# Expert 0's second layer: from plain products to Strassen's form, for its early and its late tokens

## The chip, the cores and the metric

The kernel runs on one core of one Trainium2 chip. The metric is the device time of one execution in microseconds (us), the median of several. A change under 0.5% (some 2.2 us here) can't be told from none.

Engines: PE (TensorE, the matrix engine) with its weight loads shown apart as PEld; DVE (VectorE); ACT (ScalarE); POOL (GpSimd); SP (SyncE), which issues most of the transfers. Each takes its instructions in the order of the program. DMA engines move data beside them.

## The reference

Linear attention with a decay per head, then a mixture of eight experts, top 1, over the 3072 tokens of width 512:

```python
# attention: B, H, S, D = 4, 8, 768, 64, in blocks of 64 positions
intra = ((qb @ kb.T) * Dmask) @ vb
inter = (qb * lam_pow) @ kv_state
out[block] = intra + inter
kv_state = lam_block * kv_state + (kb * rev_pow).T @ vb
# x: (3072, 512); experts: E = 8, F = 1024
logits = x @ w_gate
expert_idx = argmax(logits);  gate_w = softmax(logits)[expert_idx]
for e in range(8):
    xe = x[expert_idx == e]
    out[expert_idx == e] = gate_w * (maximum(xe @ w1[e], 0) @ w2[e])
```

All is float32.

## The kernel before

**Stages.** The attention runs in 12 steps of 128 positions and two batches. At the end of each step its tokens are routed: their rows are scattered into a list per expert in device memory (`xs`). Then the experts run one after another as "passes", each over a fixed number of tokens (`CAPS`), half of them of even and half of odd place in the list. Expert 0 has two passes: "0a" with 256 tokens that are on its list early (`passes[0]`, called `first`), begun while the attention still ends, and "0b" with the other 130 (`passes[1]`, called `second`). Passes 2 to 8 are the seven other experts, 418 down to 356 tokens.

**The two layers.** The first layer makes `hT`, the hidden values with features on the partitions: 8 chunks of 128 features by the pass's tokens. The second layer is `outputs` for pass 0a (tokens on the output's partitions; the 128 tokens of a chunk of `hT` are the weights that PE holds, 512 columns of `w2t` stream through) and `columns` for pass 0b (128x128 pieces of `w2t` are the held weights, the 130 tokens stream through). In `columns` features are on the partitions, so `put_columns` turns the result back by 32x32 blocks on DVE and writes it to memory, from where `take_rows` reads it as rows for the gates.

**Strassen's form.** Passes 2 to 8 already use it, for both layers. `form` computes a product of 2x2 blocks with seven products of blocks in place of eight. It needs four sums of blocks of each factor (S1 to S4 of the left, T1 to T4 of the right), all made by DVE: `second_sums` for `w2`, `sums_of_hidden` and `last_sum` (S4) for `hT`, `first_sums` for `w1`, `token_sums` for the tokens. Three of the products are added up in one PSUM bank, the `chain`; between them ACT copies the bank out (`snap`), and DVE joins results (`join`, `give`). The order on PE is A11·B11 (chain), A12·B21, S2·T2 (chain), S1·T1, S3·T3 (chain), S4·B22, A22·T4 (chain). `fill(j)` is called after step j, and issues whatever else the engines are to do there. `outputs_fast` is the form for the last pass, with tokens on the partitions; `columns_fast` is that for passes 2 to 7, with tokens streaming.

**What sets the order.** PE, DVE, ACT and SP issue strictly as the code is written. POOL keeps its order too for the scatters. So the order of calls in `experts()` is the order on each engine:

```python
hidden(first, w1t, range(4, FC))       # L1102: last half of 0a's first layer
outputs(first, w2t, between)           # L1109; between(): 0b's rows are cleared, turned
hidden(second, w1t)                    # L1110
prepare(passes[2])                     # L1112: turns pass 2's tokens, token_sums
w1 = first_sums(weights[1][0])         # L1113
columns(second, w2t)                   # L1118
for i in range(2, last + 1): ...       # L1119
```

`w1t` and `w2t` of expert 0 lie by columns: `w2t` is a view [128, 8 chunks, 4 groups, 128], whose groups of 128 columns are stored apart (four dimensions); those of the other experts are [128, 8, 512]. `piece` gives a 128x128 piece of either.

A float32 product of the program is two weight loads and two matmuls in the trace, each with the same shape; a turning by PE (`tr`, L678) is one of each.

Of the kernel before, what the change touches and what calls it, by code (L numbers as in the profile page):

```python
# [10 lines left out]
F32 = mybir.dt.float32  # L11
BF16 = mybir.dt.bfloat16
I32 = mybir.dt.int32
AX = mybir.AxisListType
ALU = mybir.AluOpType
# [6 lines left out]
def kernel(  # L22
# [242 lines left out]

    def piece(wt, c, g):
        return wt[:, c, g] if len(wt.shape) == 4 else wt[:, c, g * P:(g + 1) * P]

    def load_turned(w1t, d):
        for c in range(DC):  # L270
# [16 lines left out]
    def bank(i, shape, name):  # L287
        return ps.tile(shape, F32, tag=f"bank{i}", name=name)
# [372 lines left out]
    def evac(i, dst, src):  # L661
        if i % 2:
            return nc.scalar.copy(dst, src)
        return nc.vector.tensor_copy(dst, src)
# [93 lines left out]
        return left_sums(a, a[1][0], s2, s3, s4)  # L758

    def second_sums(w2t, keep):  # L760
        b = [[w2t[:, j * FC // 2:(j + 1) * FC // 2, k * MD // 2:(k + 1) * MD // 2]
              for k in range(2)] for j in range(2)]
        t1, t2, t4, *t3 = (qkv.tile([P, FC // 2, MD // 2], F32, tag=t, name=f"t_{t}")
                           for t in ("qkvq" if keep else "qkv"))
        return right_sums(b, t1, t2, t3[0] if keep else b[0][1], t4)

# [71 lines left out]
    def columns_fast(m, w2, fill):  # L838

        start_columns(m)  # L840
        mm = quarters(FC // 2, lambda lhs, rhs, fc, i: rhs[:, fc, i * P:(i + 1) * P],
                      lambda lhs, rhs, fc, i: lhs[:, fc, :])

        def give(i, k, p, u):
            to = m.yT[i][:, 2 * k:2 * k + 2, :m.h]
            if u is None:
                nc.scalar.copy(to, p)
            else:
                nc.vector.tensor_add(to, p, u)
            if (i, k) in ((0, 1), (1, 0)):  # L850
                put_columns(m, i)

        form(banks_of(form_banks, [P, 2, m.h]), mm, (m.a, w2), temps_of([P, 2, m.h]), copy_snap,
             nc.vector.tensor_add, give, fill)

    def columns(m, w2t):
        start_columns(m)
        for c in range(0, DC, 2):
            po = bank(next(po_banks), [P, 2, m.n], "po")
            for i, fc in itertools.product(range(2), range(FC)):  # L860
                nc.tensor.matmul(po[:, i, :], lhsT=piece(w2t, fc, c + i),  # L861
                                 rhs=m.hT[:, fc, :], start=(fc == 0), stop=(fc == FC - 1))
            for i in range(2):
                evac(1, m.yT[i][:, c:c + 2, :m.h], po[:, :, i * m.h:(i + 1) * m.h])
        for i in range(2):
            put_columns(m, i)

    def start_columns(m):
        m.y = []
# [35 lines left out]
                             ACT.Copy, scale=m.gates[:w, j, k:k + 1])  # L905
        scatter(m.ids[:w, j, k:k + 1], o[:w])

    def outputs_fast(m, w2t, w2):
        tail_rows(m, w2t)
        last_sum(m)  # L910

        def mm(p, lhs, rhs, first):
            for fc in range(FC // 2):
                nc.tensor.matmul(p, lhsT=lhs[:, fc, :], rhs=rhs[:, fc, :],  # L914
                                 start=(first and fc == 0), stop=(fc == FC // 2 - 1),
                                 skip_group_check=True)

        o = [work.tile([P, MD], F32, tag="kT", name="o") for i in range(2)]
        outs = [[o[i][:, k * MD // 2:(k + 1) * MD // 2] for k in range(2)] for i in range(2)]
        gate = [m.gates[:, 0, i:i + 1] for i in range(2)]  # L920
        ids = ffn.tile([P, 2], I32, name="ids_of_halves", bufs=1)
        nc.vector.tensor_scalar(out=ids[:, 0:1], in0=m.ids[:, 0, 1:2], scalar1=float(N),
                                scalar2=2.0, op0=ALU.min, op1=ALU.mult)
        nc.vector.tensor_scalar(out=ids[:, 1:2], in0=ids[:, 0:1], scalar1=1.0, scalar2=None,
                                op0=ALU.add)

        def snap(j, dst, src):
            nc.scalar.activation(dst, src, ACT.Copy, scale=gate[j == 2])

        def join(dst, p, u):  # L930
            nc.vector.scalar_tensor_tensor(out=dst, in0=p, scalar=gate[0], in1=u,
                                           op0=ALU.mult, op1=ALU.add)

        def give(i, k, p, u):
            if u is None:
                nc.scalar.activation(outs[i][k][:, :P], p[:, :P], ACT.Copy, scale=gate[i])
                nc.vector.tensor_scalar_mul(outs[i][k][:, P:], p[:, P:], gate[i])
            else:
                nc.vector.scalar_tensor_tensor(out=outs[i][k], in0=p, scalar=gate[i], in1=u,
                                               op0=ALU.mult, op1=ALU.add)  # L940
            if i == 1:
                scatter(ids[:, k:k + 1], outs[i][k], out.rearrange("n (k f) -> (n k) f", k=2))
            elif k == 1:
                scatter(m.ids[:, 0, i:i + 1], o[i])

        form(banks_of(form_banks, [P, MD // 2]), mm, (m.a, w2), temps_of([P, MD // 2]), snap, join,
             give, nothing_else)

    def tail_rows(m, w2t):

# [123 lines left out]
    def experts():  # L1074

        total = routed.total
        passes.append(make_pass(0, EARLY, CAPS[0] - EARLY, "0b"))
        load_rows(passes[1])
        for i in range(1, E):
            e = nc.values_load(routed.turns[0:1, i:i + 1], min_val=1, max_val=E - 1,  # L1080
                               engines=[mybir.EngineType.SP])
            passes.append(make_pass(e, 0, CAPS[i], str(i)))
            if i == 1:
                load_meta(passes[2])
                weights.append([load_first(e), None])
        fetch(passes[2])
        weights[1][1] = load_second(passes[2].w)
        last = len(passes) - 1

        def prepare(m):  # L1090
            turn(m)
            token_sums(m)
            for f in m.b.todo:
                f()

        def run_todo(lists, j):
            for f in lists.get(j, ()):
                f()

        w1t, w2t = weights[0]  # L1100
        first, second = passes[:2]
        hidden(first, w1t, range(4, FC))  # L1102

        def between():
            clear_rows(second, place_late, total[:, 0:1])
            turn_rows(second, (2, 3))
            know_rows(second, place_late, total[:, 0:1])

        outputs(first, w2t, between)  # L1109
        hidden(second, w1t)  # L1110
        weights.append([load_first(passes[3].w), None])
        prepare(passes[2])  # L1112
        w1 = first_sums(weights[1][0])  # L1113
        for f in w1.todo:
            f()
        load_meta(passes[3])
        fetch(passes[3])
        columns(second, w2t)  # L1118
        for i in range(2, last + 1):  # L1119
            m = passes[i]  # L1120
            take_rows(passes[i - 1])
            if i < last:
                weights[i][1] = load_second(passes[i + 1].w)
                if i + 2 <= last:
                    load_meta(passes[i + 2])
            else:
                load_tail(m)
            w2 = second_sums(weights[i - 1][1], i == last)
            rows = give_rows(passes[i - 1])
            fills = {j: [f] for j, f in zip((1, 3, 7, 9), w2.todo)}  # L1130
            slots = (10, 13) if i == 2 else (9, 10, 13, 13) if i == last else (9, 10, 13)
            for j, f in zip(slots, rows):
                fills.setdefault(j, []).append(f)
            later = rows[len(slots):]
            hidden_fast(m, w1, i == last, lambda j: run_todo(fills, j))
            know_meta(m, total[:, i - 1:i])
            if i == last:
                know_tail(m, total[:, E - 1:])
                tc.keep_in_program_order(nc.gpsimd.drain())
                outputs_fast(m, weights[i - 1][1], w2)  # L1140
                break
            if i + 2 <= last:
                weights.append([load_first(passes[i + 2].w), None])
            following = passes[i + 1]
            turn(following)
            token_sums(following)
            if i + 2 <= last:
                fetch(passes[i + 2])
            w1 = first_sums(weights[i][0])
            t, w = following.b.todo, w1.todo  # L1150
            fills = {0: later + t[:2], 1: t[2:] + w[:1], 2: [lambda m=m: last_sum(m)] + w[1:2], 3: w[2:3],
                     4: w[3:]}
            columns_fast(m, w2, lambda j: run_todo(fills, j))
# [162 lines left out]
```

## Time and profile before

| | |
|---|---|
| median of 3 runs | 431.95 us (431.32 to 432.99) |
| the profiled execution's own time | 433.69 us |
| its span, first to last instruction | 431.8 us |
| PE busy | 419.5 us, 97% of the span |
| DVE, ACT, POOL busy | 283.5, 151.5, 95.4 us |
| mean granted PE clock | 0.99 of full speed |
| pass 0a, second layer | 137.97 to 152.25 us of the span |
| pass 0b, first layer | 152.25 to 159.41 us |
| pass 0b, second layer | 159.41 to 166.58 us |
| passes 2 to 8 | 166.58 to 424.42 us |

The profile is of one execution. Its chain of work that ended last gives, for each stretch of time, the work that the end waited for; where PE stands there, what PE has to do sets the time. A row of the timeline gives start, length, engine, line, operation, shapes and the number of instructions, and in brackets how long the engine sat idle before and for what. Lengths of PE rows hold the way through the array, so neighbours overlap; the step from one row's start to the next is what an instruction costs.

### The profile page before, as it was taken

Reading aid. Unit: us, or ns where it says so; the run is one execution under the profiler, and the core shown is the slowest. Engines: PE = TensorE matmul, PEld = TensorE weight load, DVE = VectorE, ACT = ScalarE, POOL = GpSimd, SP = SyncE. Lnnn points to the kernel's source line nnn. Section 1 sums busy time; section 2 is a strip of 40 time slices with the busy share of each in tenths; the row PEclk is TensorE's granted clock in tenths of the full one; section 3 lists DMA queues with packets and bytes.
Section 4 is the critical chain, followed back from the end, with each engine's and each line's share of the span. In section 5 each row is a group of like instructions: output and inputs, shape, how many; then the busy total and the mean of one; then the engine's idle time right before and its main releaser. Section 6 shows DMA issues by size and latency. Waiting matters only on the chain.

```text
span 431.8 us, 11052 instructions
## 1 busy us (share of the span) xinstructions
PE 419.5 (97%) x4407; PEld 389.6 (90%) x4407; DVE 283.5 (66%) x678; ACT 151.5 (35%) x370; POOL 95.4 (22%) x122
## 2 busy tenths in 40 slices
PE   8899999999999999999999999999999999999993
PEld 4689999999887499999999999999999999999672
DVE  4677777777744229787569576766957958766601
ACT  3355546555541022430351144025124314413420
POOL 6526545551324000000011003001101200300402
PEclk9899999999999999999999999999999999999997
DMA  9999899988883699764399069539927927604301
GB/s 198 227 214 263 226 250 234 234 211 218 235 268 125 224 332 296 248 233 73 87 330 297 15 185 352 157 85 312 301 44 246 356 49 192 217 0 98 114 26 56
DMA packets 129373, 84.50 MB, mean 196 GB/s; under 512 B 81764, under 2 KB 112244, under 8 KB 129312
## 3 DMA queue, kind: packets, MB, share of 16 engines
q1 hardware_dynamic: 122752, 69.56, 59.0%
q0 software_dynamic: 4464, 13.62, 8.8%
q8 instruction: 37, 0.61, 0.6%
q10 hardware_dynamic: 2096, 0.52, 0.5%
q14 instruction: 24, 0.20, 0.1%
HBM read 64.58 MB, written 19.42 MB: 195 GB/s over the span
## 4 chain that ended last, share of the span: by engine, by line
PE 94%; DVE 2%; DMA 1%; ACT 1%; issue 0%; POOLq 0%; POOL 0%; ACTq 0%
PE p L804 55%; PE tx L450 6%; PE ph L690 5%; PE po L973 3%; PE op L412 3%; PE sp L370 3%; PE p L914 3%; PE tq L313 3%; PE op L390 2%; PE cp L429 2%; PE tk L331 2%; PE op L404 2%; PE po L861 2%; PE po L957 2%; PE sp L375 1%; DMA lam_bc<-in_lam_dram 1%
## 5 line engine op out<-in xcount | busy, mean ns | idle before, releaser
L655 POOL DMA_INDIRECT out_dram<-o,ids x13 | 12.9, 990 | 172.4 <-ACT o L903 170.2
L804 PE MATMUL p<-hT,w2t 128*128 128x209 f32 (+5 forms) x288 | 49.4, 327 | 0.0
L804 PEld LDWEIGHTS p<-hT,w2t 128*128 128x128 f32 x288 | 47.7, 189 | 0.0
L731 ACT COPY u_qsT<-p 128x418 f32<-128x418 f32 (+6 forms) x40 | 19.2, 480 | 77.6 <-PE p L804 76.3
L804 PE MATMUL p<-xgT,w1t 128*128 128x209 f32 (+6 forms) x224 | 38.7, 326 | 0.0
L804 PEld LDWEIGHTS p<-xgT,w1t 128*128 128x128 f32 x224 | 36.7, 190 | 0.0
L829 ACT ACTIVATE hT<-hT 128x418 f32<-128x418 f32 (+6 forms) x42 | 22.0, 525 | 32.9 <-DVE hT L828 32.9
L507 POOL DMA_INDIRECT xs<-x,row x24 | 23.6, 985 | 39.6 <-DVE slot L545 13.9
L380 DVE TENSOR_TENSOR mt<-sp,tables 128x384 f32<-128x384 f32 x48 | 23.6, 549 | 3.4 <-PE sp L375 3.1
L450 PE MATMUL tx<-back,xT 128*128 128x136 f32 x192 | 25.3, 285 | 0.0
L450 PEld LDWEIGHTS tx<-back,xT 128*128 128x128 f32 x192 | 23.1, 190 | 0.8
L828 DVE TENSOR_TENSOR hT<-p,u_qsT 128x418 f32<-128x418 f32 (+6 forms) x28 | 15.5, 558 | 12.2 <-ACT u_qsT L731 9.6
L690 PE MATMUL ph<-xgT,w1t 128*128 128x256 f32 (+1 forms) x128 | 22.0, 328 | 0.2 <-issue 0.2
L690 PEld LDWEIGHTS ph<-xgT,w1t 128*128 128x128 f32 x128 | 19.2, 190 | 2.6 <-issue 0.9
L716 DVE TENSOR_TENSOR u_qsT<-p,u_qsT 128x418 f32<-128x418 f32 (+6 forms) x20 | 11.2, 560 | 15.4 <-PE p L804 15.4
L370 PE MATMUL sp<-qT,kT 64*64 64x128 f32 x384 | 19.8, 276 | 1.4 <-DVE qsT L323 0.8
L804 PE MATMUL p<-t_kd,w1t 128*128 128x209 f32 (+6 forms) x112 | 20.7, 327 | 0.0
L804 PE MATMUL p<-t_xT,s_q 128*128 128x209 f32 (+6 forms) x112 | 20.6, 326 | 0.0
L804 PE MATMUL p<-t_sd,w1t 128*128 128x209 f32 (+6 forms) x112 | 20.5, 326 | 0.0
L804 PE MATMUL p<-xgT,s_v 128*128 128x209 f32 (+6 forms) x112 | 20.5, 326 | 0.0
L804 PE MATMUL p<-xgT,s_k 128*128 128x209 f32 (+6 forms) x112 | 20.5, 326 | 0.0
L670 DVE STREAM_TRANSPOSE xgT<-xb 128x768 f32<-128x768 f32 (+1 forms) x14 | 13.7, 1014 | 10.0 <-PE ph L690 9.9
(239 smaller groups left out, 902.9 us busy)
## 6 DMA issues: line engine op xcount, KB each, us to landing
w1t<-in_moe_w_dram SPq DMA_DIRECT2D x7, 2048.0 KB
w2t<-in_moe_w_dram SPq DMA_DIRECT2D x7, 2048.0 KB
qkv_in<-in_q_dram SPq DMA_DIRECT2D x12, 256.0 KB
q_in<-in_q_dram SPq DMA_DIRECT2D x12, 256.0 KB
y<-ye SPq DMA_DIRECT2D x6, 512.0 KB
xb<-xs SPq DMA_DIRECT2D x32, 96.0 KB
xb<-xs SPq DMA_DIRECT2D x24, 112.0 KB
ye<-yb SPq DMA_DIRECT2D x12, 224.0 KB
```

Source lines behind the costliest of these rows:

```text
L313: nc.tensor.transpose(tq[:, a, b], m.q[:, u, at:at + 2], ident)
L370: nc.tensor.matmul(sp[r][halves[u], b, u:u + 2], lhsT=m.kT[u][halves[r], a, b, halves[u]], rhs=m.qT[u][halves[r], a, b, :], start=(b == 0) ...
L380: nc.vector.tensor_mul(mt[:, r], sp[r], decay[:, r, a].unsqueeze(1).to_broadcast(shp))
L412: nc.tensor.matmul(out_at(m, a, b, u, r)[:, D:], lhsT=m.v[:, u, column(b, a, r), :], rhs=m.mt[a][:, r, b, 2 * u], start=False, stop=(m.n = ...
L450: nc.tensor.matmul(tx[:, b * W:(b + 1) * W], lhsT=m.xT[hp % 2][:, hp // 2, b, :], rhs=back[:, hp, b * E:b * E + W], start=(b == 0), stop=( ...
L507: put = tc.keep_in_program_order(nc.gpsimd.indirect_dma_start(out=xs, out_offset=bass.IndirectOffsetOnAxis(ap=row, axis=0), in_=src, in_of ...
L670: nc.vector.transpose(m.xgT[:, :, i, :].rearrange("p d (b t) -> p b d t", t=Q), m.xb[:, i * nb:(i + 1) * nb].rearrange("p b (d f) -> p b d ...
L690: nc.tensor.matmul(ph, lhsT=piece(w1t, dc, fc), rhs=m.xgT[:, dc].rearrange("p k h -> p (k h)"), start=(dc == 0), stop=(dc == DC - 1))
L731: nc.scalar.copy(dst, src)
L804: nc.tensor.matmul(p[:, i, :], lhsT=lhs_of(lhs, rhs, c, i), rhs=rhs_of(lhs, rhs, c, i), start=(first and i == 0 and c == 0), stop=(c == ch ...
L828: nc.vector.tensor_add(outs[i][k], p, u)
L829: nc.scalar.activation(outs[i][k], outs[i][k], ACT.Relu)
```

## The change

Expert 0's second layer goes through `form` in both passes. `outputs_fast` no longer calls `tail_rows` and `last_sum` itself (its old caller does), and can scatter whole rows for both halves; `columns` is gone, and `columns_fast` takes pass 0b. `second_sums` makes T1 to T4 of expert 0's `w2t` once (`keep`: T3 gets a buffer of its own), for both passes. `half_of` takes halves of the four-dimensional tile. And `first_sums` of pass 2's `w1` is moved ahead of `prepare(passes[2])`, which now stands behind pass 0b's `sums_of_hidden`.

```diff
+    def half_of(wt, j, k):
+        rows = slice(j * FC // 2, (j + 1) * FC // 2)
+        if len(wt.shape) == 4:
+            return wt[:, rows, 2 * k:2 * k + 2]
+        return wt[:, rows, k * MD // 2:(k + 1) * MD // 2]
...
     def second_sums(w2t, keep):
-        b = [[w2t[:, j * FC // 2:(j + 1) * FC // 2, k * MD // 2:(k + 1) * MD // 2]
-              for k in range(2)] for j in range(2)]
-        t1, t2, t4, *t3 = (qkv.tile([P, FC // 2, MD // 2], F32, tag=t, name=f"t_{t}")
+        b = [[half_of(w2t, j, k) for k in range(2)] for j in range(2)]
+        t1, t2, t4, *t3 = (qkv.tile(list(b[0][0].shape), F32, tag=t, name=f"t_{t}")
                            for t in ("qkvq" if keep else "qkv"))
...
     def columns_fast(m, w2, fill):
-        mm = quarters(FC // 2, lambda lhs, rhs, fc, i: rhs[:, fc, i * P:(i + 1) * P],
+        mm = quarters(FC // 2, lambda lhs, rhs, fc, i: piece(rhs, fc, i),
                       lambda lhs, rhs, fc, i: lhs[:, fc, :])
...
-    def outputs_fast(m, w2t, w2):
-        tail_rows(m, w2t)
-        last_sum(m)
+    def outputs_fast(m, w2, banks, by_halves=False, fill=nothing_else):
...
-            if i == 1:
+            if i == 1 and by_halves:
                 scatter(ids[:, k:k + 1], outs[i][k], out.rearrange("n (k f) -> (n k) f", k=2))
-            elif k == 1:
+            elif (i, k) in ((0, 1), (1, 0)):
                 scatter(m.ids[:, 0, i:i + 1], o[i])
...
+        def clear():
+            clear_rows(second, place_late, total[:, 0:1])
         def between():
-            clear_rows(second, place_late, total[:, 0:1])
             turn_rows(second, (2, 3))
             know_rows(second, place_late, total[:, 0:1])
-        outputs(first, w2t, between)
+        w2 = second_sums(w2t, True)
+        t = w2.todo
+        t[0]()
+        t[2]()
+        sums_of_hidden(first, slice(0, FC // 2), True)
+        fills = {1: t[1:2], 2: [lambda: last_sum(first)], 3: [clear] + t[3:], 5: [between]}
+        outputs_fast(first, w2, itertools.cycle([7, 4, 5, 1]),
+                     fill=lambda j: run_todo(fills, j))
         hidden(second, w1t)
         weights.append([load_first(passes[3].w), None])
-        prepare(passes[2])
         w1 = first_sums(weights[1][0])
         for f in w1.todo:
             f()
+        sums_of_hidden(second, slice(0, FC // 2), False)
+        prepare(passes[2])
         load_meta(passes[3])
         fetch(passes[3])
-        columns(second, w2t)
+        fills = {2: [lambda: last_sum(second)]}
+        columns_fast(second, w2, lambda j: run_todo(fills, j))
```

**Pass 0a on PE.** The rows below are PE's program around pass 0a's second layer: line, operation, result<-streamed,held, shape of the result and number of products. First before, then now (`ph` is a first layer, `po` and `p` are second layers, `tr` the turning of pass 0b's rows; `s_h` and `s_mt` are sums of `hT`, `t_q`, `t_k`, `t_v` sums of the weights).

```order
L690 MATMUL ph<-xgT,w1t 128x256 x16
L973 MATMUL po<-w2t,hT 128x512 x12
L678 MATMUL tr<-impulse,xg 128x65 x8
L973 MATMUL po<-w2t,hT 128x512 x4
L690 MATMUL ph<-xgT,w1t 128x130 x32
```

```order
L696 MATMUL ph<-xgT,w1t 128x256 x16
L905 MATMUL p<-w2t,hT 128x256 x8
L905 MATMUL p<-t_k,s_h_3063 128x256 x4
L905 MATMUL p<-t_q,s_h_3062 128x256 x4
L905 MATMUL p<-t_q,s_mt 128x256 x4
L905 MATMUL p<-w2t,s_mt 128x256 x4
L684 MATMUL tr<-impulse,xg 128x65 x8
L905 MATMUL p<-t_v,hT 128x256 x4
L696 MATMUL ph<-xgT,w1t 128x130 x32
```

Sixteen products of 512 columns have become 28 of 256, and the turning stands ahead of the last group of four.

**Pass 0b on PE.** PE's program from the end of pass 0b's first layer to the start of pass 2, before and now.

```order
L690 MATMUL ph<-xgT,w1t 128x130 x32
L861 MATMUL po<-hT,w2t 128x130 x32
L804 MATMUL p<-xgT,w1t 128x209 x8
L804 MATMUL p<-t_xT,s_q 128x209 x4
L804 MATMUL p<-t_sd,w1t 128x209 x4
```

```order
L696 MATMUL ph<-xgT,w1t 128x130 x32
L809 MATMUL p<-hT,w2t 128x65 x16
L809 MATMUL p<-s_h_3208,t_k 128x65 x8
L809 MATMUL p<-s_h_3207,t_q 128x65 x8
L809 MATMUL p<-hT,t_q 128x65 x8
L809 MATMUL p<-s_h_3208,w2t 128x65 x8
L809 MATMUL p<-hT,t_v 128x65 x8
L809 MATMUL p<-xgT,w1t 128x209 x8
```

Thirty-two products that stream 130 columns have become 56 that stream 65; each still holds a 128x128 piece of weights.

**Pass 0b on DVE.** DVE's program in the same place, before and now (`s_k`, `w1t`, `s_q`, `s_v` are `first_sums`; `xgT<-xb` turns pass 2's tokens, and `t_sd`, `xgT`, `t_xT`, `t_kd` are its `token_sums`; `s_h`, then `hT`, are pass 0b's sums).

```order
L600 COPY gates_0b<-xg 80x2
L670 STREAM_TRANSPOSE xgT<-xb 128x7x4x32 x2
L752 TENSOR_TENSOR t_sd<-xgT 128x418
L752 TENSOR_TENSOR xgT<-xgT 128x2x209
L752 TENSOR_TENSOR t_xT<-xgT,t_sd 128x418
L752 TENSOR_TENSOR t_kd<-xgT,t_xT 128x418
L752 TENSOR_TENSOR s_k<-w1t 128x1024
L749 TENSOR_TENSOR w1t<-w1t 128x2x512
L752 TENSOR_TENSOR s_q<-w1t 128x1024
L752 TENSOR_TENSOR s_v<-w1t,s_q 128x1024
```

```order
L758 TENSOR_TENSOR s_v<-w1t,s_q 128x1024
L795 TENSOR_TENSOR s_h_3207<-hT 128x260
L796 TENSOR_TENSOR s_h_3208<-s_h_3207,hT 128x260
L797 TENSOR_TENSOR hT<-hT 128x4x65
L676 STREAM_TRANSPOSE xgT<-xb 128x7x4x32 x2
L758 TENSOR_TENSOR t_sd<-xgT 128x418
L758 TENSOR_TENSOR xgT<-xgT 128x2x209
L758 TENSOR_TENSOR t_xT<-xgT,t_sd 128x418
L758 TENSOR_TENSOR t_kd<-xgT,t_xT 128x418
L867 MEMSET yT 128x4x31 x2
L854 TENSOR_TENSOR yT<-p,u_qT 128x2x65
L802 TENSOR_TENSOR s_h_3208<-hT,s_h_3208 128x260
```

The four sums of `w1` now come first, then three sums of pass 0b's hidden values, then pass 2's tokens, and behind these `last_sum` (the last row), which the product S4·B22 needs.

More of the change, by code (lines that the diff above doesn't have):

```diff
@@ L854, in columns_fast @@
              nc.vector.tensor_add, give, fill)
[L856 to L866, printed above, removed]
     def start_columns(m):
@@ L920, in outputs_fast @@
         gate = [m.gates[:, 0, i:i + 1] for i in range(2)]
[L921 to L925, printed above, removed]
+        if by_halves:
+            ids = ffn.tile([P, 2], I32, name="ids_of_halves", bufs=1)
+            nc.vector.tensor_scalar(out=ids[:, 0:1], in0=m.ids[:, 0, 1:2], scalar1=float(N),
+                                    scalar2=2.0, op0=ALU.min, op1=ALU.mult)
+            nc.vector.tensor_scalar(out=ids[:, 1:2], in0=ids[:, 0:1], scalar1=1.0, scalar2=None,
+                                    op0=ALU.add)
         def snap(j, dst, src):
@@ L940, in give @@
                                                op0=ALU.mult, op1=ALU.add)
-            if i == 1:
+            if i == 1 and by_halves:
                 scatter(ids[:, k:k + 1], outs[i][k], out.rearrange("n (k f) -> (n k) f", k=2))
-            elif k == 1:
+            elif (i, k) in ((0, 1), (1, 0)):
                 scatter(m.ids[:, 0, i:i + 1], o[i])
-        form(banks_of(form_banks, [P, MD // 2]), mm, (m.a, w2), temps_of([P, MD // 2]), snap, join,
-             give, nothing_else)
+        form(banks_of(banks, [P, MD // 2]), mm, (m.a, w2), temps_of([P, MD // 2]), snap, join,
+             give, fill)
     def tail_rows(m, w2t):
@@ L1139, in experts @@
                 tc.keep_in_program_order(nc.gpsimd.drain())
-                outputs_fast(m, weights[i - 1][1], w2)
+                tail_rows(m, weights[i - 1][1])
+                last_sum(m)
+                outputs_fast(m, w2, form_banks, by_halves=True)
                 break
```

## The prediction

> **What bounds the kernel now.** I read the page's head first, then the chain of waits, then the timeline of each engine between 126 and 170 us, where the change lies, and last the length of single instructions by line.
>
> ```profile
> span 431.8 us, 11052 instructions
> PE 419.5 (97%) x4407; PEld 389.6 (90%) x4407; DVE 283.5 (66%) x678; ACT 151.5 (35%) x370; POOL 95.4 (22%) x122
> ...
> 130.87 7.10 PE ph L690 x32
> 137.97 10.30 PE po L973 x24
> 148.27 0.49 PE tr L678 x8
> 148.76 3.49 PE po L973 x8
> 152.25 7.16 PE ph L690 x64
> 159.41 7.16 PE po L861 x64
> 166.58 238.54 PE p L804 x1456
> ```
>
> PE is busy 97% of the span, and the chain goes from one PE group to the next with no gap: a microsecond that PE needs more or less between 130 and 170 us moves all that follows. The other engines count only where PE would have to wait for them. So the question is what PE pays for the new products, and whether DVE delivers their sums in time.
>
> What one PE instruction costs is read from steps and from first instructions:
>
> ```profile
> L914 PEld LDWEIGHTS p<-w2t,hT x16: 186/190/190, 412.1 to 415.2; 128*128 128x128 f32 x16
> L914 PE MATMUL p<-w2t,hT x16: 379/379/483, 412.1 to 415.4; 128*128 128x256 f32 x16
> L957 PEld LDWEIGHTS po<-w2t,hT x32: 121/125/125, 405.0 to 411.1; 128*50 128x50 f32 x32
> L957 PE MATMUL po<-w2t,hT x32: 592/592/632, 405.0 to 411.5; 128*50 128x512 f32 x32
> L678 PEld LDWEIGHTS tr<-impulse,xg x16: 138/142/143, 118.9 to 148.5; 128*128 128x128 f32 x8, 65*128 65x128 f32 x8
> 415.61 1.89 PE L914 MATMUL p<-t_k,s_h 128*128 128x256 f32 x8
> 422.52 1.89 PE L914 MATMUL p<-t_v,hT 128*128 128x256 f32 x8
> ```
>
> The three numbers are shortest, median and longest in ns. The first matmul of a group, whose weight load nothing hides, is 483 - 379 = 104 ns longer than its fellows where 128 columns of weights are loaded, and 632 - 592 = 40 ns where 50 are. The loads' own lengths say the same: 190 and 125 ns, 65 ns for 78 columns. So a float32 load occupies the load path some 0.83 ns a column, 104 to 107 ns for 128, and otherwise runs beside the matmul ahead of it. The load of a turning is shorter (142 ns for 128 columns, 48 less).
>
> **Pass 0a on PE.** Removed: 16 products, 32 matmuls of 512 columns. Added: 28 products, 56 matmuls of 256. The last two rows above are four groups of eight apart: 6.91 / 4 = 1.73 us a group, 216 ns each, far above a load's 107, so the loads stay hidden. Seven groups are 12.09 us. The eight turnings (0.49) remain. The stage was 137.97 to 152.25, 14.28 us; it becomes 12.58. **-1.70 us**, if nothing is late.
>
> **Is anything late in pass 0a?** DVE gets four weight sums, four sums of hidden values, four joins and half a gate in place of one gate. Rows for these, and for the gap in which they fall:
>
> ```profile
> 136.45 0.16 DVE L1071 TENSOR_REDUCE beyond<-beyond 128x1 int32<-128x8 int32 x1
> 138.01 0.38 ACT L693 ACTIVATE hT<-ph 128x256 f32<-128x256 f32 x1 [1.34 <-PE ph L690]
> 144.88 0.75 DVE L980 TENSOR_SCALAR o<-po,gates_0a 128x512 f32<-128x512 f32 x1 [8.26 <-PE po L973]
> 145.54 0.35 DVE L609 TENSOR_SCALAR lim<-place_late,total 80x2 f32<-80x2 f32 x2
> 145.93 1.22 DVE L612 TENSOR_SCALAR xg<-xg,lim 80x512 f32<-80x512 f32 x2
> 163.92 1.22 DVE L752 TENSOR_TENSOR s_k<-w1t 128x1024 f32<-128x1024 f32 x1
> 405.15 0.69 DVE L790 TENSOR_TENSOR s_h<-hT 128x512 f32<-128x512 f32 x1 [0.57 <-ACT hT L829]
> 415.88 0.48 DVE L939 SCALAR_TENSOR_TENSOR o<-p,meta,u_qT 128x256 f32<-128x256 f32 x1 [6.89 <-PE p L914]
> 414.09 0.47 ACT L928 ACTIVATE u_qT<-p,meta 128x256 f32<-128x256 f32 x1 [0.47 <-PE p L914]
> ```
>
> DVE sat idle 8.26 us there. From 136.6: T1 and T2 (1.22 each) to 139.0; S1, S2 (0.69 each; the last ReLU ended 138.4) to 140.4. PE wants S2·T2 after two groups each of A11 and A12, at 137.97 + 3.46 = 141.4. Slack 1.0. S3, a join (p is there at 141.4), T3, S4: 143.8, wanted at 144.9 and 146.6. The join of S1·T1 waits for PE until 144.9, ends 145.4; clearing pass 0b's rows (0.35 + 1.22; they had landed by 145.93, when DVE cleared them without a wait) to 147.0; T4 to 148.2. PE wants the cleared rows at 148.3, T4 behind the turnings at 148.8. Slack 1.3 and 0.6, the thinnest; a late T4 would cost what it is late, a few tenths. ACT's new copies (0.47) fit between groups of 1.73. The turned rows, copied out in under half a us, have the last group's 1.73 to hide in (3.49 before). I cost all this at 0, between 0 and +0.5. POOL's scatters keep their order and number; SP's list is unchanged row for row.
>
> **Pass 0b on PE.** Removed: 64 matmuls that stream 130 columns, 7.16 us, 111.9 ns each. Added: 112 that stream 65, in the same two-load, two-matmul form, each with a load of 128 columns. No row has this shape. Bounds:
>
> ```profile
> 148.11 0.66 PE L678 MATMUL tr<-impulse,xg 65*128 65x65 f32 x8
> 169.24 1.58 PE L804 MATMUL p<-t_xT,s_q 128*128 128x209 f32 x8
> 170.66 1.58 PE L804 MATMUL p<-t_sd,w1t 128*128 128x209 f32 x8
> ```
>
> If only the stream counted: 209 columns cost 1.42 / 8 = 177 ns, 0.85 a column, 55 ns for 65; and the eight turnings with 65 streamed columns took 0.49 / 8 = 61 ns each, with their short loads. From above: the same loads kept up with 111.9 ns a matmul in the removed lines, so they can't need more. Between 61 and 112 I take **110 ns**, because each load occupies 104 to 107 ns and the turnings show that a few ns come on top (61 against 55). The matmul's 55 then hides under the load, not the other way round. 112 x 0.110 = 12.32 us against 7.16: **+5.16 us** (at 61 ns 6.83, -0.33; at 112 ns 12.54, +5.38). Seven eighths of the streaming, but seven quarters of the weight loads.
>
> The Trainium skill, "TensorE: Matmul & The Clock Gate", section "LDWEIGHTS (loading the stationary operand)", speaks against the change in the same way: a load takes its columns divided by 1.2, whatever the rows, 107 ns for 128 (by that alone, as an estimate, 112 loads are 11.9 us, and pass 0b costs 4.8 more). The trace agrees for float32 products (104) and not for turnings, which load 128 columns within steps of 61 ns.
>
> **Is anything late in pass 0b?** DVE, after pass 0a:
>
> ```profile
> 152.25:159.41 7.16, 7.16 (x67) 7.16 (x66) 0.00 (x0) 2.65 (x8) 0.99 (x1) 1.00 1.13 301
> 143.82 0.40 SPq L252 DMA_DIRECT2D w1t<-in_moe_w_dram  x1
> 147.88 5.19 SPq L650 DMA_DIRECT2D xb<-xs  x8
> 143.80:156.00 12.20, 12.20 (x62) 7.83 (x61) 3.04 (x9) 2.04 (x6) 2.00 (x2) 1.00 0.97 275
> 148.80 0.43 DVE L664 COPY xgT<-tr 128x260 f32<-128x260 f32 x1 [1.65 <-PE tr L678]
> 159.45 0.28 ACT L693 ACTIVATE hT<-ph 128x130 f32<-128x130 f32 x1 [0.61 <-PE ph L690]
> 159.51 2.10 DVE L670 STREAM_TRANSPOSE xgT<-xb 128x896 f32<-128x896 f32 x2 [9.88 <-PE ph L690]
> 168.89 0.30 DVE L874 MEMSET yT<- 128x124 f32 x2
> ```
>
> (The windows' columns are the stretch, its length, busy time of PE, PEld, DVE, ACT, POOL, the clock, DMA share and GB/s.) During pass 0b's first layer DVE did nothing at all: that covers the 4 x 1.22 = 4.88 us of `first_sums` that now stand there, if `w1` is in. It is issued at 143.82, ahead of the tokens (`xb`); at 275 GB/s its 2.1 MB take 7.6 us, so it is in at about 152, or at 156 if the 0.9 MB of tokens share the way (3.0 MB of the 3.36 moved by then). The new first layer runs 150.55 to 157.7. `first_sums`: 152 to 156.9; the last ReLU ends about 158.3; S1, S2 at 0.43 each (260 columns) to 159.2; PE wants S2 after 32 matmuls, 157.7 + 3.5 = 161.2. Slack 2. Then S3, `prepare` (163.92 - 159.51 = 4.41), memset, one join, S4: 165.1. PE wants S4 after 80 matmuls, at 166.5. Slack 1.4. Cost 0. Pass 2 starts at 157.7 + 12.3 = 170.0 in place of 166.58; its tokens and weight sums are ready by 164.
>
> **The sum.** -1.70 + 5.16 = +3.46 us. The profiled execution took 433.69 us (1.9 beyond its span, and 1.74 above the median of the runs, even above their highest, 432.99); it would become 437.2. Against the median of 431.95: **435.4 us**, 0.8% slower.
>
> **The rivals.**
>
> A, slower still: `first_sums` stand ahead of pass 0b's sums on DVE, so a late `w1` holds up S2 and PE. It decides from a landing after 161.2 - 0.86 - 4.88 = 155.5, and costs what is beyond: 0.5 us at 156, 2.5 at 158: up to 437.9. For it: DMA is full there (share 0.97). Against it: `w1` is first in its queue.
>
> B, not slower: the loads do not bind, and a matmul of 65 columns costs the turnings' 61 ns. For it: that row. Against it: 104 ns of exposed load. Then DVE is the bound: S4 at 165.1, behind `prepare`, is wanted at 157.7 + 80 x 0.061 = 162.6; PE waits 2.5, and the last 32 matmuls end at 167.1, 0.5 later than before: 432.5, no change. The point: below about 92 ns a matmul S4 sets the end. The Trainium skill, same page, section "Back-to-back issue gap", gives an isolated matmul columns over 2.4 plus 2.5 ns, about 57 for two passes over 65 columns by my estimate; it warns in the same place that this leaves the weight load out.
>
> C, faster: B with S4 in time. 112 x 0.061 = 6.83, pass 2 at 164.5, -2.05: 429.9. Against it: DVE's order.
>
> **How the numbers follow.** The forecast has 0.78, because three rows (first matmuls, load lengths, the 112 ns of the removed lines) agree on what a load occupies; its own range is 434.4 to 436.6 (106 to 112 ns, 0 to 0.5 of lateness, the spread of the runs). A has 0.09, B 0.09, C 0.04. The range 433.9 to 437.6 takes in most of A and leaves out B and C. A difference under 0.5% (2.16 us) can't be told from none: slower than that are the forecast but for 0.02, and A, 0.85; within it B, half of C and those 0.02, 0.13; faster 0.02.
>
> **What would show it.** In the profile after: pass 0a's 56 matmuls in steps of 216 ns and its stage at 12.6 us; pass 0b's 112 matmuls at 106 to 112 ns, PEld busy throughout, its stage 12 to 12.6 us; no PE wait for DVE in either; pass 2's first product 3 to 4 us later in the span. Wrong would be: steps near 61 ns in pass 0b (B or C), PE idle ahead of S2·T2 there (A), or ahead of A22·T4 in pass 0a.

## The result, and the profile after

The changed kernel takes 436.61 us (median of 5 runs, 435.76 to 438.51) against 431.95 (431.32 to 433.0) on the same chip: ratio 1.010, 95% interval 1.0072 to 1.0128. It is slower: the medians are 4.7 us apart, the ratio gives 4.3, with 3.1 to 5.5 as the interval's ends. The two profiled executions are 3.47 us apart (437.16 and 433.69), their spans 3.4 (435.2 and 431.8).

The chain of waits of the changed kernel, in order of time (start, length, what), where pass 0a's second layer is L905 and everything in `form` with streaming tokens is L809:

```profile
137.88 10.36 PE p L905 x48
148.24 0.49 PE tr L684 x8
148.74 1.78 PE p L905 x8
150.52 7.16 PE ph L696 x64
157.68 18.34 PE p L809 x145
```

Pass 0a's second layer starts where it did (137.88, 137.97 before) and ends 1.73 us earlier, at 150.52. It took 12.64 us in place of 14.28. From there on PE is on the chain all the way, and it waits for nobody. Pass 0b is inside the last row. PE's timeline opens it (a row's start, the instructions' shapes and number):

```profile
157.51 3.68 PE L809 MATMUL p<-hT,w2t 128*128 128x65 f32 x32
161.03 1.95 PE L809 MATMUL p<-s_h,t_k 128*128 128x65 f32 x16
162.82 1.95 PE L809 MATMUL p<-s_h,t_q 128*128 128x65 f32 x16
164.61 1.95 PE L809 MATMUL p<-hT,t_q 128*128 128x65 f32 x16
166.40 1.95 PE L809 MATMUL p<-s_h,w2t 128*128 128x65 f32 x16
168.18 1.95 PE L809 MATMUL p<-hT,t_v 128*128 128x65 f32 x16
169.97 3.04 PE L809 MATMUL p<-xgT,w1t 128*128 128x209 f32 x16
160.98 1.87 PEld L809 LDWEIGHTS p<-s_h,t_k 128*128 128x128 f32 x16
```

From start to start a group of 16 takes 1.79 us, 112 ns a matmul, in every group: what 130 columns cost before (111.9). The stage runs from 157.51 to pass 2's first matmul at 169.97, 12.46 us, against 7.16: +5.30. No row has a wait in brackets. The last row is the weight loads of one group: 16 loads of 190 ns in 1.87 us, one over the other.

Two groups of pass 0a on PE, DVE, and the transfers and scatters that DVE's work hangs on:

```profile
141.17 1.89 PE L905 MATMUL p<-t_k,s_h 128*128 128x256 f32 x8
148.57 1.95 PE L905 MATMUL p<-t_v,hT 128*128 128x256 f32 x8
139.72 0.69 DVE L796 TENSOR_TENSOR s_h<-s_h,hT 128x512 f32<-128x512 f32 x1
146.60 1.21 DVE L758 TENSOR_TENSOR t_v<-w2t,t_k 128x1024 f32<-128x1024 f32 x1
154.46 1.23 DVE L758 TENSOR_TENSOR s_k<-w1t 128x1024 f32<-128x1024 f32 x1 [3.15 <-DMA w1t<-in_moe_w_dram]
159.84 0.43 DVE L796 TENSOR_TENSOR s_h<-s_h,hT 128x260 f32<-128x260 f32 x1
165.35 0.41 DVE L802 TENSOR_TENSOR s_h<-hT,s_h 128x260 f32<-128x260 f32 x1
136.53 1.23 DVE L758 TENSOR_TENSOR t_q<-w2t 128x1024 f32<-128x1024 f32 x1
136.66 1.94 POOL L513 DMA_INDIRECT xs<-nothing,row_end  x1 [0.30 <-issue]
138.90 1.03 POOL L513 DMA_INDIRECT xs<-nothing,row_end  x1 [0.30 <-issue]
141.91 0.83 SPq L645 DMA_DIRECT2D xg<-xs  x2
```

Pass 0b's S2 (L796) was ready at 160.27, wanted by PE at 161.03; S4 (L802) at 165.76, wanted at 166.40. Both in time, by 0.76 and 0.64 us. `first_sums` did wait for `w1` until 154.46. And one of POOL's scatters took 1.94 us beside T1, where the same one had taken 0.96 in the kernel before:

```profile
136.75 0.96 POOL L507 DMA_INDIRECT xs<-nothing,row_end  x1 [0.30 <-issue]
```

What follows the scatters on SP is issued 0.95 us later than before (141.91, 140.96).

### The profile page after: what moved, and what is told of

Its sections match the earlier page's. It is cut to its first block, busy times and chain, and to the rows that moved or that the text cites. A ratio compares the mean times of both kernels' runs of the same rounds, so it can differ in the third digit from the quotient of the medians.

```text
span 435.2 us, 11230 instructions
## 1 busy us (share of the span) xinstructions
PE 421.0 (97%) x4479; PEld 398.1 (91%) x4479; DVE 294.3 (68%) x698; ACT 152.5 (35%) x373; POOL 96.7 (22%) x122
## 4 chain that ended last, share of the span: by engine, by line
PE 94%; DVE 2%; DMA 1%; ACT 1%; issue 1%; POOLq 0%; POOL 0%; ACTq 0%
PE p L809 58%; PE p L905 6%; PE tx L456 6%; PE ph L696 5%; PE op L418 3%; PE sp L376 3%; PE tq L319 3%; PE op L396 2%; PE cp L435 2%; PE tk L337 2%; PE op L410 2%; PE po L949 2%; PE sp L381 1%; DMA lam_bc<-in_lam_dram 1%; DVE tables L206 1%
## 5 line engine op out<-in xcount | busy, mean ns | idle before, releaser
L809 PE MATMUL p<-hT,w2t 128*128 128x209 f32 (+6 forms) x320 | 53.0, 322 | 0.0
L809 PEld LDWEIGHTS p<-hT,w2t 128*128 128x128 f32 x320 | 51.3, 190 | 0.0
L737 ACT COPY u_qsT<-p 128x418 f32<-128x418 f32 (+7 forms) x42 | 19.7, 470 | 85.8 <-PE p L809 84.5
L809 PE MATMUL p<-xgT,w1t 128*128 128x209 f32 (+6 forms) x224 | 38.8, 326 | 0.0
L809 PEld LDWEIGHTS p<-xgT,w1t 128*128 128x128 f32 x224 | 36.8, 190 | 0.0
L722 DVE TENSOR_TENSOR u_qsT<-p,u_qsT 128x418 f32<-128x418 f32 (+7 forms) x21 | 11.5, 546 | 15.9 <-PE p L809 15.9
L873 DVE STREAM_TRANSPOSE yb<-yT 128x896 f32<-128x896 f32 (+2 forms) x14 | 13.7, 978 | 10.5 <-ACT yT L852 10.2
L809 PE MATMUL p<-t_kd,w1t 128*128 128x209 f32 (+6 forms) x112 | 20.6, 326 | 0.0
L809 PE MATMUL p<-t_xT,s_q 128*128 128x209 f32 (+6 forms) x112 | 20.6, 326 | 0.0
L809 PE MATMUL p<-t_sd,w1t 128*128 128x209 f32 (+6 forms) x112 | 20.5, 326 | 0.0
L809 PE MATMUL p<-xgT,s_v 128*128 128x209 f32 (+6 forms) x112 | 20.5, 326 | 0.0
L809 PE MATMUL p<-xgT,s_k 128*128 128x209 f32 (+6 forms) x112 | 20.5, 326 | 0.0
```

The lines of the kernel that those rows point to most:

```text
L809: nc.tensor.matmul(p[:, i, :], lhsT=lhs_of(lhs, rhs, c, i), rhs=rhs_of(lhs, rhs, c, i), start=(first and i == 0 and c == 0), stop=(c == ch ...
L873: nc.vector.transpose(m.yb[:, i * nb:(i + 1) * nb], m.yT[i].rearrange("p d (b t) -> p b d t", t=Q))
```

## The experiments

The theory: a 65-column matmul costs what its own weight load occupies, with the few ns on top that the prediction allowed, 112 ns; pass 0b's form pays for 112 loads in place of 64, and all else in the change is worth its -1.7 us. The rivals: the sums on DVE, or the change as a whole, cost it; or it is some fixed cost of an instruction.

**Pass 0b's form alone.** Pass 0a by plain products again; the weights' sums, all four, stand ahead of them on DVE:

```diff
-        t[0]()
-        t[2]()
-        sums_of_hidden(first, slice(0, FC // 2), True)
...
-        outputs_fast(first, w2, itertools.cycle([7, 4, 5, 1]),
-                     fill=lambda j: run_todo(fills, j))
+        for f in t:
+            f()
...
+        outputs(first, w2t, both)        # both(): clear(), between()
```

> Pass 0b in Strassen's form, pass 0a in plain products as before. Theory (a 65-column matmul costs what its weight load occupies, 112 ns): pass 0b's second layer takes 12.5 us against 7.16, the kernel 5.3 us more than before, 437.3 us, ratio 1.012. Rival (the loss comes from the whole change together, the sums of pass 0a's form crowding DVE, and pass 0b's form alone would cost little): within 1.5 us of before.

Measured: 437.5 us, ratio 1.0112 (1.0080 to 1.0144). Its PE rows show the same groups:

```profile
157.15 3.68 PE L809 MATMUL p<-hT,w2t 128*128 128x65 f32 x32
160.67 1.95 PE L809 MATMUL p<-s_h,t_k 128*128 128x65 f32 x16
169.60 3.04 PE L809 MATMUL p<-xgT,w1t 128*128 128x209 f32 x16
```

157.15 to 169.60 is 12.45 us, as in the changed kernel, and pass 0a's form is not in this run. The rival falls.

**Half the streamed columns, the same loads.** In the kernel before, `columns` streams the first 65 of the 130 tokens over the same 64 loads:

```diff
-                nc.tensor.matmul(po[:, i, :], lhsT=piece(w2t, fc, c + i), rhs=m.hT[:, fc, :], ...)
+                nc.tensor.matmul(po[:, i, :m.h], lhsT=piece(w2t, fc, c + i), rhs=m.hT[:, fc, :m.h], ...)
...
```

> The kernel before, with plain products in pass 0b that stream 65 columns in place of 130: the products of half of pass 0b's tokens are left out, all 64 weight loads stay. Theory (the load of 128 float32 columns occupies 107 to 112 ns and sets the step): still 112 ns a matmul, 7.16 us, the same time as before, 431.95 within 0.5 us. Rival (the streamed columns set the step, and the form was slow for another reason): 61 ns a matmul, 3.9 us, so 3.2 us less than before, 428.7.

Measured: 431.73 us, ratio 0.9993 (0.9971 to 1.0015). Half the work on the same loads saves nothing:

```profile
157.67 7.25 PE L861 MATMUL po<-hT,w2t 128*128 128x65 f32 x64
164.77 3.04 PE L804 MATMUL p<-xgT,w1t 128*128 128x209 f32 x16
```

Sixty-four in 7.10 us, 111 ns each. Strassen's form has no part in this run: the step is that of the load, or at least of the load and matmul as a pair, not of the columns.

**The same loads in two halves.** To tell the load from a fixed cost of an instruction, each product becomes two with 64 columns of weights, whose results lie in the two halves of the PSUM partitions. That is twice as many instructions for the same arithmetic:

```diff
...
+            for i, fc, at in itertools.product(range(2), range(FC // 2), halves):
+                nc.tensor.matmul(p[at, i, :], lhsT=piece(rhs, fc, i)[:, at], rhs=lhs[:, fc, :], ...)
...
```

> The changed kernel, but each product of pass 0b's form is made in two with 64 columns of weights each, for the two halves of PE's columns (224 matmuls in place of 112, same arithmetic). Theory (a load occupies 0.83 ns a column of its half, and the two halves load at once, as in the attention's products of 64 columns, 29.5 ns a matmul): 224 x 0.030 = 6.7 us of PE; then DVE's S2 (ready 160.3 in the changed kernel's profile, wanted at 159.4) and S4 (ready 165.8, wanted at 163) end last, so PE idles some 3 us and pass 2 starts at 167.7 in place of 170.0: 2.3 us less than the changed kernel. Rival 1 (a fixed 112 ns an instruction): 25 us, 12.6 us more. Rival 2 (the halves load one after the other): 224 x 0.06 = 13.4 us, 1 us more.

Measured: 434.6 us against 432.41, ratio 1.0048 to before (1.0024 to 1.0071): 2.2 us over before, where the changed kernel's median was 4.7 over.

```profile
155.85 2.09 PE L849 MATMUL p<-hT,w2t 128*64 128x65 f32 x64
158.50 1.16 PE L849 MATMUL p<-s_h,t_k 128*64 128x65 f32 x32 [0.57 <-DVE s_h L796]
159.45 1.14 PE L849 MATMUL p<-s_h,t_q 128*64 128x65 f32 x32
163.91 1.15 PE L849 MATMUL p<-s_h,w2t 128*64 128x65 f32 x32 [2.38 <-DVE s_h L802]
165.92 3.10 PE L809 MATMUL p<-xgT,w1t 128*128 128x209 f32 x16
```

From 158.50 to 159.45 are 32 matmuls, 30 ns each: a quarter of 112 for half of the columns of weights. So it is no fixed cost of an instruction; loads of 64 columns into different halves run at once, and so do their matmuls. The stage takes 10.07 us (155.85 to 165.92) in place of 12.46. DVE is now late at two places: S2 by 0.57 us, and S4, which rival B of the prediction had named, by 2.38.

**Those two sums made early.** On top of the halves, S1 to S4 of pass 0b stand ahead of pass 2's tokens on DVE:

```diff
-        for f in w1.todo:
+        for f in w1.todo[:3]:
             f()
         sums_of_hidden(second, slice(0, FC // 2), False)
+        last_sum(second)
         prepare(passes[2])
+        w1.todo[3]()
...
-        fills = {2: [lambda: last_sum(second)]}
-        columns_fast(second, w2, lambda j: run_todo(fills, j))
+        columns_fast(second, w2, nothing_else)
```

> The halves of e4, and on DVE S1 to S4 of pass 0b behind three of w1's four sums and ahead of pass 2's tokens (the fourth behind these). Theory (in e4 PE idled 0.57 us for S2 and 2.38 for S4, and nothing else held it): both waits go, pass 0b's second layer takes 6.6 to 6.8 us against 7.16 in plain products, and the kernel is 1.7 + 0.4 = 2.1 us faster than before, ratio 0.995, 3 us faster than e4. Rival (pass 2's tokens, now later, hold up pass 2's first layer): PE idles there instead, and the time stays near e4's, over before's.

Measured: 433.28 us, ratio 0.9989 (0.9950 to 1.0028), where 0.995 was expected. The stage took 8.33 us (158.64 to 166.97), not 6.6 to 6.8. In this run S4 was written over S2 (they share a buffer) before the product with S2, which therefore waited for it (0.16 us) and used S4: the kernel leaves out the true S2·T2. And PE sat idle once more, for nothing that the profile shows:

```profile
165.18 0.86 PE L849 MATMUL p<-s_h,w2t 128*64 128x65 f32 x23 [1.04 <-issue]
```

The next run gives S4 a buffer of its own.

> The halves with S4 of pass 0b in a buffer of its own and made early, S2 left whole. The order of e5 wrote S4 over S2 ahead of S2's product, and its PE also idled 1.04 us for nothing that the profile shows amid the 224 small matmuls. Theory: no wait for DVE in pass 0b; the products take 224 x 0.030 = 6.7 us, plus that idle time if it comes with the number of PE's instructions: pass 0b's second layer 6.7 to 7.8 us against 7.16 in plain products, the kernel 1.1 to 2.2 us under before, ratio 0.995 to 0.9975. Rival (pass 2's tokens, now later on DVE, hold PE up): PE waits for DVE at pass 2's first products, ratio 1.0 or more.

Measured: 432.69 us, ratio 1.0008 (0.9989 to 1.0027), where 0.995 to 0.9975 was expected. The waits for DVE are gone, as the theory has it, but not all of the idle time:

```profile
159.27 2.09 PE L849 MATMUL p<-hT,w2t 128*64 128x65 f32 x64
163.98 0.40 PE L849 MATMUL p<-s,w2t 128*64 128x65 f32 x8
165.44 0.92 PE L849 MATMUL p<-s,w2t 128*64 128x65 f32 x24 [1.05 <-issue]
167.22 3.09 PE L809 MATMUL p<-xgT,w1t 128*128 128x209 f32 x16
```

The stage is 159.27 to 167.22, 7.95 us, against 7.16 in plain products: the 1.05 us in which PE waits for nothing that the profile shows eat what the form saves. It stood at the same place in the run before, amid the same group.

The traces say more of it than the profile's rows. Six idle times of PE of this kind stand in the eleven profiles: these two, 0.71 and 1.25 us in the attention of the changed kernel, 0.18 in its second profile and 0.22 in the kernel before. Counted through PE's list in the trace (loads, matmuls and what its sequencer does), all six begin after 4033, 5313 or 6081 instructions, which are whole multiples of 256 apart. Each ends 1.15 to 1.58 us after the end of a transfer of 16384 bytes on the queue that the profile calls "instruction". So PE seems to have run out of instructions there, at the end of a block of 256. In this run that block lasted 4.96 us, and 3.91 without the idle time; the transfer ahead of its end had begun 2.65 us into the block and taken 0.93. Products of 30 ns use up a block faster than those of 112, so they are the likelier to meet this; that is argued from the traces, and no run tried it.

From pass 0a's second layer to pass 2 this kernel takes 27.85 us against 28.60, so it should still be 0.75 us under before; the comparison, with an interval of 0.8 us either way around +0.35, shows no gain.

**Pass 0a's form alone**, pass 0b and the order on DVE as before, twice:

> Pass 0a in Strassen's form, pass 0b in plain products, pass 2's tokens ahead of the sums of w1, both as before. Theory: pass 0a's second layer 12.6 us in place of 14.3, nothing lost elsewhere: 1.7 us less than before, ratio 0.996. Rival (the sums of the form make PE wait, or the slower scatter on POOL delays what follows, and the gain is given back): within 0.5 us of before, or slower.

> Pass 0a's form alone once more, beside e7 on the same chip: 1.7 us under before, ratio 0.996, within 0.7 us of e7 either way.

Measured: ratio 0.9960 (0.9931 to 0.9990), 1.7 us less, and, on another chip, 0.9975 (0.9948 to 1.0002), 1.1 us less. The second was to lie within 0.7 us of the run with halves and S4 of its own; it came out 1.3 under it (431.38, 432.69), because that run had not gained what was expected of it. Chain of waits of the first:

```profile
137.94 10.36 PE p L917 x48
148.30 0.49 PE tr L684 x8
148.80 1.78 PE p L917 x8
150.58 7.16 PE ph L696 x64
157.74 7.16 PE po L866 x64
```

12.64 us for pass 0a again, 7.16 for pass 0b: the part of the change that pays, and the best kernel of the study. The stage shows the gain of 1.64 us; of the whole time it is under 0.5%, and the second interval just reaches 1.

**T1 and T2 behind S1 to S3 on DVE**, in the changed kernel, for the slow scatter:

```diff
-        t[0]()
-        t[2]()
         sums_of_hidden(first, slice(0, FC // 2), True)
+        t[0]()
+        t[2]()
```

> The changed kernel with T1 and T2 of expert 0's weights on DVE behind pass 0a's S1 to S3 instead of ahead of them. The profile of the changed kernel has a POOL scatter of 1.94 us beside T1 (0.96 before), and the read of pass 0b's rows issued 0.95 us later. Theory (DVE's sum of 1024 columns holds up POOL's scatter beside it): the scatters at 135 to 139 are 0.96 again and the read is issued at 141.0; the slow scatter, if any, moves with T1. T2 is then ready at 143 and wanted at 141.2, so PE idles near 1.5 us there and the span is that much longer. Rival (chance, or another cause): a scatter of 1.9 us stays where it was.

Measured in a single execution: 437.49 us, span 435.7.

```profile
135.04 0.96 POOL L513 DMA_INDIRECT xs<-nothing,row_end  x1 [0.30 <-issue]
136.31 0.96 POOL L513 DMA_INDIRECT xs<-nothing,row_end  x1 [0.30 <-issue]
139.25 0.83 SPq L645 DMA_DIRECT2D xg<-xs  x2
151.84 1.73 POOL L661 DMA_INDIRECT out_dram<-o,ids_0a  x1 [1.54 <-DVE o L929]
151.48 1.22 DVE L758 TENSOR_TENSOR s_k<-w1t 128x1024 f32<-128x1024 f32 x1
138.66 1.22 DVE L758 TENSOR_TENSOR t_q<-w2t 128x1024 f32<-128x1024 f32 x1
141.35 1.97 PE L905 MATMUL p<-t_k,s_h 128*128 128x256 f32 x8 [1.63 <-DVE t_k L758]
```

All scatters into `xs` take 0.96 us once none begins beside a weight sum, and PE waits 1.63 us for T2, as expected. Here it is a scatter of results that begins beside the first sum of `w1`, and it takes 1.73 us in place of 1.00. (The attention ended 1.6 us earlier in this execution, so its span hides part of that.) With the four sums in a row, in the run of pass 0b's form alone, two scatters took 1.94 and 1.96.

**The changed kernel again.**

> The changed kernel once more, on the same chip as the two above. The stages' sum (1.64 us won in pass 0a, 5.3 lost in pass 0b) gives 3.6 us over before; the first comparison gave 4.7, with 3.1 to 5.5 as its interval. Theory (the rest is spread of the runs): 3 to 4.5 us over before. Rival (a steady loss elsewhere of 1 us): 4.5 to 5.5.

Measured: 438.79 us, ratio 1.010 (1.0066 to 1.0133): 4.3 us more, the interval from 2.9 to 5.8. It does not settle what it was meant to, for both theory and rival lie within the interval.

## Why the prediction was right, and where its sizes were off

**Pass 0a, -1.70 us.** 12.64 us measured, -1.64 (the next stage 1.73 earlier), and the run with this part alone bears it out. The thinnest slacks were those of S2 and T4, 0.76 us each: S2 was ready at 140.41 and wanted at 141.17, T4 ready at 147.81 and wanted at 148.57. The prediction had 1.0 and 0.6.

**Pass 0b, +5.16 us.** The step was that of the loads, as forecast from the first matmul of a group, from the loads' lengths and from the removed lines: 112 ns for 110, 12.46 us for 12.32, +5.30. The half-stream run shows it without Strassen's form, the run in halves with twice the instructions. The rule of the Trainium skill, "TensorE: Matmul & The Clock Gate", section "LDWEIGHTS (loading the stationary operand)", agrees with 107 ns as the load's own time; another 5 ns a step came on top. Its rule that the columns count, not the rows, fits the lengths of the float32 products' loads: 190 ns for 128 columns, 138 for 64, and 133 for 64 columns of only 64 rows.

**Cost 0 for waits.** Right, though with less room than worked out: S2 of pass 0b had 0.8 us, not 2, and S4 0.64, not 1.4, since `w1` was in at 154.46, not 152. That is the term I mis-sized. I divided its bytes by the mean rate of the stretch, 7.6 us, and let it start at once; it took 9.7 us from issue to landing, which lies between that and the case I had named of the tokens sharing the way. And the 0.95 us that SP lost behind the slow scatter was not in it at all (POOL's scatters I had put down as unchanged). Had `w1` come 0.8 us later, rival A would have begun.

**Rival B** fell on its premise, but its second half, that S4 behind `prepare` would then set the end, came true in the run with halves, where two halves together take about the 61 ns of the rival. It had put 2.5 us of PE's time down to S4; PE lost 2.38 there, and 0.57 before it to S2, of which the rival had said nothing, so 2.95 in all.

**The sum.** +3.46 forecast; the profiled executions are 3.47 apart, pass 2's first matmul 3.56 (169.97, 166.41). That the first two agree to 0.01 us is luck. Pass 0b alone was 0.14 us off its forecast, and the profiled executions differ by far more in the attention, before pass 0a's second layer: it began between 135.9 us (the run of pass 0b's form alone) and 139.5 (the last one with halves). The medians are 4.7 us apart, the two ratios give 4.3, and both intervals hold 3.5; the median of 436.61 lies at the upper end of the forecast's own range, 434.4 to 436.6.

Whether the changed kernel loses a steady microsecond elsewhere stays open, but the traces say where it could be. From pass 2's first product to the last instruction all eleven profiled executions take 265.2 to 265.5 us, so it is not in what follows pass 0b. By the ratios, the seven comparisons of kernels with pass 0a's form come out from 0.1 us under to 1.1 over what their stages between pass 0a's second layer and pass 2 give, the two of kernels without it 0.2 to 0.5 under. That hints at a loss ahead of pass 0a's second layer that comes with its form; of the seven, only that of the last run with halves is clear of its interval by itself.

## What to carry to other kernels

Before halving a matmul's streamed columns, compare what is left with its weight load: in these float32 products, with 128 columns of weights, a step costs 112 ns whether 65 or 130 columns stream. A form with fewer products but more loads pays only where each still streams enough: 256 columns in pass 0a, 12% less time; 65 in pass 0b, 74% more. My estimate of the point between, from these steps and 0.85 ns a streamed column, is some 115: there seven quarters as many steps of 112 ns cost what plain products of 230 columns do. No run tried it. The load's own time could be read from the profile of before: the first matmul of a group, whose load nothing hides, was 104 ns longer than the next. Where the load binds, two loads of 64 columns into different halves of the array run side by side (30 ns a matmul here), and what comes next, here DVE's sums and then PE's idle time of 1.05 us, has to be counted against the gain.

## What the runs showed of the hardware that I had not expected

- A POOL scatter (its instruction, not its data) that began beside a DVE sum of two SBUF operands, 1.23 us long, took 1.94 us in place of 0.96, in all eight executions where T1 stood there, and 0.96 in the one where T1 was moved. In the changed kernel it ended 0.84 us after T1 did, and the scatter of 1.73 us ended 0.87 us after its sum. A scatter that had begun 0.41 us before a sum (136.31, S1 at 136.72, in the run with T1 moved) took 0.96, and the sum its usual 0.69. The Trainium skill, "SBUF — State Buffer", section "SBUF: two separate sides", has DVE and POOL share a pair of ports that the one which starts first holds for its whole instruction, also where DVE has two SBUF operands and POOL's instruction reads SBUF, as the scatter reads `row_end`. The trace agrees for a scatter that comes second. It does not show the other half: no sum was longer for a scatter that had begun before it (S1 above; T2 took 1.23 us while the scatter of 1.94 still ran).
- PE idled 1.04 and 1.05 us at the same instruction amid 64-column products, in the two executions where it did not wait for DVE there. All six idle times of this kind begin at a whole number of blocks of 256 instructions from one another and end 1.15 to 1.58 us behind a transfer on the queue "instruction". Fetching of PE's instructions is the likely cause; no run tried it.
